# The first four blocks in chunks of 64, with earlier weight loads and a product on two blocks' columns

## The chip, the cores and the metric

The kernel runs on one core of a Trainium2 chip. The metric is the device time of one execution in microseconds (us). The engines of the core work side by side, each from its own queue: PE (TensorE; matmuls, with the weight loads shown as PEld), DVE (VectorE), ACT (ScalarE), POOL (GpSimd), and SP, which issues most of the DMA transfers. They wait for one another by semaphores.

## The reference

```python
# q, k, v: (batch 8, heads 8, seq 576, head_dim 64)
scores = scale * np.matmul(q, k.transpose(0, 1, 3, 2))
gamma = 1.0 - 2.0 ** (-5.0 - np.arange(H, dtype=np.float32))
Dmat = np.where(rel >= 0, gamma[:, None, None] ** rel[None, :, :], 0.0)   # rel = row - column
attn = np.matmul(scores * Dmat[None], v)
x = attn.transpose(0, 2, 1, 3).reshape(B * S, H * D)                       # (4608, 512)
h = np.maximum(np.maximum(x @ w1, x @ w2), x @ w3)                         # d_ff 768
out = h @ w_out                                                            # (4608, 512)
```

The four weight matrices come as 64-bit floats and are turned into 32-bit floats on the chip; q, k and v are 32-bit. No softmax is taken, so attention can be run as a recurrence: a block of tokens needs its own scores and a state, the decayed sum of key times value over all earlier tokens of its sequence.

## The kernel before

**Tiling.** The 4608 tokens are cut into 36 blocks of 128 tokens, four to a tile of 512 (CPT is 4). `ffn(t)` turns the xT of a tile (the attention's result, transposed, 512 columns) into outputs. The hidden size of 768 is six pieces of 128 columns (fb), taken as three pairs (fp). A unit is a pair and one of w1, w2, w3, in the order (fp, i) = (0, 0), (0, 1), (0, 2), (1, 0) and so on. Tile 0 uses plain products: `up_plain(t, h, fb, i)` multiplies one weight piece by the 512 columns of xT in four matmuls, and `maximum` takes the result to h, on ACT for w1 and on DVE, as a maximum, for w2 and w3. Later tiles use formulas with fewer products, which the change does not touch.

**Attention of a block, first four blocks.** `load` fetches k, q and v (256 KB each, SP's queue). `decay` multiplies v by a factor for each row into vd, on POOL for blocks 0 to 2 and on DVE for block 3. `transposes` makes kT and qT on PE, and ACT copies them out of PSUM. `scores` multiplies whole blocks of 128 by 128 for each head (L308); DVE multiplies by the causal mask (st, L311). `state` forms the key-value sums of the block (kv, L421); `keep` adds the old state and multiplies by a factor (L429 to L432). `values` multiplies the masked scores by vd (L462) and adds the old state times q (L477); `output` scales the result into xT on DVE. Helper `soon` runs the DVE steps, so those show line L220.

**Attention of blocks 4 to 7.** `parity_scores` and `parity_values` split a block into two chunks of 64 tokens, and the heads by parity, so that all products are 64 by 64 by 64 (L321, L326, L504, L495). There are two states to a block, the one after its first chunk (mids) and the one after its second (states). The products with the old state are issued in two halves, `old(0)` and `old(1)`. Between them, ACT copies one column of each of the two PSUM tiles into a scrap tile `first` (L508), which holds `old(1)` back until `old(0)` has landed. These four blocks have their place between the products of tile 0.

**Weights.** `load_weights(n)` issues the next n pieces, two DMAs of 256 KB each. `convert_all` is a generator which turns pieces into 32-bit floats in small steps; `convert(n)` runs its next n steps. For a piece they are exponent (one step on DVE, L773, one on ACT, L775), fraction (L781, L782, L784), whole (L787), sign and product (L791, L799; only then may PE use it). The first pair goes piece by piece; the second and the third do exponent and fraction of both pieces first, then whole, sign and product of each; from the fourth on, a pair is one operation.

**Order.** The order on every engine is written out by hand: an engine's queue is the order in which the program issues. The opening (from L1056) loads in the order block 0, block 1, k and q of block 2, piece 0, v of block 2, k and q of block 3, piece 1, v of block 3, then four pieces, and works through blocks 0 to 3. `first_ups`, the first unit of tile 0, contains the rest of block 3: it issues the first piece of w1 on the 384 columns of blocks 0 to 2, then block 3's key-value sums and values, then the second piece on 384 columns, then both on the last 128.

Of the kernel before, what the change touches and what calls it, by code (L numbers as in the profile page):

```python
# [48 lines left out]
C = 128  # L49
# [49 lines left out]
def kernel(  # L99
# [160 lines left out]
    def decay(g):  # L260
        factor = gk[:].unsqueeze(2).to_broadcast([C, H, D])
        t = raws.pop(("v", g))
        if spread or g >= CPT + 2:
            vds[g] = t
            scaling.extend(partial(nc.scalar.mul, t[:, h, :], t[:, h, :], gk[:, h:h + 1]) for h in range(H))
            return
        vds[g] = vpool.tile([C, H, D], FP32, tag="s", name="vd")
        engine = nc.gpsimd if g < CPT - 1 else nc.vector
        engine.tensor_tensor(vds[g][:], t[:], factor, op=ALU.mult)
# [4 lines left out]
    def transposes(g, names="kq"):  # L274
# [14 lines left out]
        for n in names:  # L289
            src = raws["k", g] if n == "k" else raws.pop(("q", g))  # L290
            pool, tag = (ps_r, "r") if g >= CPT else (ps_x, "x")
# [5 lines left out]
    def scores(g):  # L297
        chore(len(urgent))
        scale(len(scaling))
        if g >= CPT:  # L300
            (chunk_scores if g >= BY_CHUNKS else parity_scores)(g)
            return
        qT, kT = qks[g]["q"], qks[g]["k"]
        s = [ps_r.tile([C, NP, C], FP32, tag="r", name=f"s{j}") for j in range(2)]
        for p in range(NP):
            for j in range(2):
                r = slice(D * j, D * (j + 1))
                nc.tensor.matmul(s[j][:, p, :], lhsT=kT[r, p, :], rhs=qT[r, p, :], start=True, stop=True)  # L308
        for j in range(2):
            st = sts[g, j] = att.tile([C, NP, C], FP32, tag=f"m{j}", name="st", bufs=2 + j)  # L310
            soon(partial(nc.vector.tensor_tensor, st[:], s[j][:],  # L311
                         causal[:].unsqueeze(1).to_broadcast([C, NP, C]), op=ALU.mult))

    def parity_scores(g):

        qT, kT, kr, vd = qks[g]["q"], qks[g]["k"], raws.pop(("k", g)), vds[g]
# [7 lines left out]
        def key_value(p, j, c):  # L324
            if c in kept:
                nc.tensor.matmul(rows[c][half(j), 1, p, :], lhsT=kr[half(c), 2 * p + j, :],  # L326
                                 rhs=vd[half(c), 2 * p + j, :], start=True, stop=True)

        for p in range(NP):
            for n in range(2):  # L330
                score(p, 0, n)
                score(p, 1, 1 - n)
                key_value(p, 1 - n, 0)
                key_value(p, n, 1)
# [21 lines left out]
        for c in kept:  # L356
            (states if c else mids)[g + c] = ppool.tile([P, NP, D], FP32, tag="part", name="state")
            soon(partial(keep_parity, c))

    def begins(g):  # L360
        return g + 1 < NG and start_of(g + 1) != 0
# [51 lines left out]
    def state(g):  # L413

        kr = raws["k", g]
        kvs[g] = None
        if begins(g):
            r = start_of(g) or 0
            kvs[g] = ps_r.tile([P, NP, D], FP32, tag="r", name="kv")
            for h in range(H):  # L420
                nc.tensor.matmul(kvs[g][half(h % 2), h // 2, :], lhsT=kr[r:, h, :], rhs=vds[g][r:, h, :],  # L421
                                 start=True, stop=True)

    def keep(g):
        factor = gs[:].unsqueeze(2).to_broadcast([P, NP, D])

        def step(t, kv):
            if start_of(g) is not None:
                nc.vector.tensor_tensor(t[:], kv[:], factor, op=ALU.mult)  # L429
            else:  # L430
                nc.vector.tensor_tensor(t[:], kv[:], states[g][:], op=ALU.add)
                (nc.gpsimd if g < CPT - 2 else nc.vector).tensor_tensor(t[:], t[:], factor, op=ALU.mult)  # L432

        if begins(g):
            t = states[g + 1] = ppool.tile([P, NP, D], FP32, tag="part", name="state")
            soon(partial(step, t, kvs[g]))

# [6 lines left out]
    def values(chunks, new_states=(), later=False, middle=()):  # L444

        def before(g):
            return C if start_of(g) is None else start_of(g)

        chore(len(urgent))
        t, i = divmod(chunks[0], CPT)
        if chunks[0] >= CPT:
            (chunk_values if chunks[0] >= BY_CHUNKS else parity_values)(chunks, t, i)
            return
        pool, tag = (ps_r, "r") if chunks[0] >= CPT - 1 else (ps_y, "y")
        o = [pool.tile([P, len(chunks), NP // 2, C], FP32, tag=tag, name="o") for _ in range(2)]
        for m, g in enumerate(chunks):
            for n in range(NP):
                for c in range(2):  # L460
                    h = head(c, n)
                    nc.tensor.matmul(o[n % 2][half(c), m, n // 2, :], lhsT=vds[g][:, h, :],  # L462
                                     rhs=sts[g, h % 2][:, h // 2, :], start=m == 0 and n < 2,
                                     stop=before(g) == 0, skip_group_check=True)
        for g in new_states:
            if g not in kvs:
                state(g)
        for step in middle:
            step()
        for m, g in enumerate(chunks):  # L470
            old = before(g)
            if old > 0:
                for n in range(NP):
                    for c in range(2):
                        h = head(c, n)
                        r = half(h % 2)
                        nc.tensor.matmul(o[n % 2][half(c), m, n // 2, :old], lhsT=states[g][r, h // 2, :],  # L477
                                         rhs=qks[g]["q"][r, h // 2, :old], start=False, stop=True,
                                         skip_group_check=True)
        finish = partial(output, chunks, o, t, i)  # L480
        if later:
            return finish
        finish()

    def parity_values(chunks, t, i):
        o = [ps_r.tile([P, len(chunks), NP, D], FP32, tag="r", name="o") for _ in range(2)]
# [20 lines left out]
        for m in range(2):  # L507
            nc.scalar.copy(first[:], o[m][:, 0, 0, 0:1])  # L508

        def rest():  # L510
            old(1)
            between.append(partial(chunk_output, o, chunks, t, i))

        between.append(rest)
# [22 lines left out]
    def chunk_output(o, chunks, t, i):  # L537
# [3 lines left out]
        for m in range(2):  # L541
            soon(partial(nc.vector.tensor_tensor, x[:, :, :, m], o[m][:],
                         gq[:, :, half(m)].unsqueeze(1).to_broadcast([P, 2, NP, D]), op=ALU.mult))
        sums_of_x(t, i + len(chunks) - 1)

    def output(chunks, o, t, i):
        if i == 0:
            xT[t] = xpool.tile([P, NDC, NT], FP32, tag="xT", name="xT")
        for b in range(2):
            shape = [P, NP // 2, len(chunks), C]  # L550
            soon(partial(
                nc.vector.tensor_tensor,
                xT[t][:, b::2, i * C:(i + len(chunks)) * C].rearrange("p u (m c) -> p u m c", c=C),
# [651 lines left out]
```

## Time and profile before

| | us |
|---|---|
| median of 3 runs (lowest, highest) | 741.54 (741.34, 741.76) |
| the profiled execution | 741.6 |
| its span in the trace | 739.6 |
| PE busy | 734.1 |
| DVE busy | 576.1 |
| ACT busy | 345.0 |
| PE's first product of the second unit, from the span's start | 30.82 |

The profile comes from one execution. Its own time is 2.0 us longer than the span of the instructions in the trace. Busy times of the engines overlap, so they don't add up to the span. A row of a timeline has the start, the time to the end of the last instruction merged into it, the engine, the line, the operation, what it writes and reads, and how many instructions it stands for. A 32-bit matmul of the program shows as two instructions on PE, called passes here. Times within the text are from the start of the span.

### The profile page before, as it was taken

The page shows a single profiled execution, that of the slowest core. Times are in us where ns is not written, and L with a number is a line of the kernel's source. Part 1 is how long each engine was busy: PE and PEld are TensorE (multiplying, and loading weights), DVE is VectorE, ACT ScalarE, POOL GpSimd, SP SyncE. Part 2 cuts the span into 40 slices and gives each one's busy share as a digit, 9 for nine tenths or more (in the row PEclk, how much of TensorE's full clock was granted, in tenths as well). Part 3 has the DMA queues.
Part 4 walks back from the last instruction along what each step waited for, and adds up shares of the span by engine and source line. Part 5 has one row for each costly group of instructions (what it writes and reads, how often), then busy time and mean ns, then how long its engine had stood idle before and what let it go on. Part 6 is the DMA issues. An engine that isn't in the chain of part 4 may idle for free.

```text
span 739.6 us, 17315 instructions
## 1 busy us (share of the span) xinstructions
PE 734.1 (99%) x6948; PEld 605.8 (82%) x6948; DVE 576.1 (78%) x1066; ACT 345.0 (47%) x731; POOL 33.8 (5%) x42
## 2 busy tenths in 40 slices
PE   8999999999999999999999999999999999999998
PEld 7654556888888888888888888888888888888887
DVE  5998897999886895699668876787768966893676
ACT  4674824454245534544354525543455255424441
POOL 2000000102000100000000000000100010000000
PEclk9999999999999999999999999999999999999999
DMA  9999533415242515141424243332514151000001
GB/s 209 249 245 268 116 59 83 89 21 96 66 85 42 97 36 105 39 83 44 109 51 75 49 107 60 59 58 58 115 22 95 39 106 30 1 31 29 0 1 57
DMA packets 226640, 58.85 MB, mean 80 GB/s; under 512 B 207872, under 2 KB 225280, under 8 KB 226560
## 3 DMA queue, kind: packets, MB, share of 16 engines
q1 hardware_dynamic: 225584, 57.71, 35.8%
q8 instruction: 54, 0.88, 0.5%
q14 instruction: 26, 0.21, 0.1%
q10 hardware_dynamic: 976, 0.04, 0.1%
HBM read 48.27 MB, written 9.44 MB: 78 GB/s over the span
## 4 chain that ended last, share of the span: by engine, by line
PE 97%; SPq 1%; DMA 1%; DVE 0%; issue 0%
PE a L905 20%; PE b L905 17%; PE c L905 9%; PE up L930 8%; PE di L750 7%; PE d L905 6%; PE e L905 6%; PE dhc L750 5%; PE deg L750 3%; PE sk L376 3%; PE down L917 3%; PE o L526 2%; PE dfd L750 2%; PE o L533 2%; PE dx L657 1%; SPq L258 1%
## 5 line engine op out<-in xcount | busy, mean ns | idle before, releaser
L893 DVE TENSOR_TENSOR part<-part 128x512 f32<-128x512 f32 x168 | 117.8, 701 | 86.2 <-ACT part L890 83.6
L890 ACT COPY part<-b 128x512 f32<-128x512 f32 x120 | 70.4, 586 | 163.5 <-PE b L905 163.5
L893 DVE TENSOR_TENSOR h<-h,part 128x512 f32<-128x512 f32 x120 | 83.2, 693 | 24.5 <-ACT h L890 20.5
L890 ACT COPY part<-a 128x512 f32<-128x512 f32 x96 | 56.3, 586 | 51.6 <-PE a L905 51.1
L208 ACT ACTIVATE vraw<-vraw,gk 128x64 f32<-128x64 f32 x240 | 76.8, 347 | 0.1
L905 PE MATMUL b<-s,n 128*128 128x256 f32 x288 | 73.9, 379 | 0.0
L930 PE MATMUL up<-xT,w 128*128 128x512 f32 (+2 forms) x160 | 64.2, 554 | 0.0
L905 PEld LDWEIGHTS b<-s,n 128*128 128x128 f32 x288 | 54.7, 190 | 7.4
L930 PEld LDWEIGHTS up<-xT,w 128*128 128x128 f32 x160 | 28.5, 190 | 29.4 <-issue 26.3
L905 PE MATMUL c<-xT,w 128*128 128x256 f32 x192 | 51.2, 389 | 0.0
L739 ACT COPY k<-di 128x256 f32<-128x256 f32 x49 | 18.2, 372 | 68.4 <-PE di L750 43.4
L905 PE MATMUL d<-s,w 128*128 128x256 f32 x192 | 49.8, 380 | 0.0
L905 PE MATMUL a<-xT,w 128*128 128x256 f32 x192 | 49.3, 379 | 0.0
L905 PE MATMUL b<-xT,n 128*128 128x256 f32 x192 | 49.3, 379 | 0.0
L905 PE MATMUL a<-s,w 128*128 128x256 f32 x192 | 49.3, 379 | 0.0
L393 POOL TENSOR_TENSOR s<-s,gs_of 64x512 f32<-64x512 f32 x21 | 22.5, 1072 | 558.1 <-DVE s L391 441.7
L905 PE MATMUL e<-xT,w 128*128 128x256 f32 x192 | 45.4, 379 | 0.0
L905 PE MATMUL a<-xT,n 128*128 128x256 f32 x192 | 45.4, 379 | 0.0
L905 PEld LDWEIGHTS e<-xT,w 128*128 128x128 f32 x192 | 36.5, 190 | 5.4 <-issue 0.5
L905 PEld LDWEIGHTS a<-xT,w 128*128 128x128 f32 x192 | 36.5, 190 | 5.0
L905 PEld LDWEIGHTS a<-s,w 128*128 128x128 f32 x192 | 36.5, 190 | 5.0
L905 PEld LDWEIGHTS b<-xT,n 128*128 128x128 f32 x192 | 36.5, 190 | 5.0
(200 smaller groups left out, 1378.2 us busy)
## 6 DMA issues: line engine op xcount, KB each, us to landing
bits<-in_moe_w_dram SPq DMA_DIRECT2D x36, 256.0 KB, 5.7
kraw<-in_k_dram SPq DMA_DIRECT2D x32, 256.0 KB, 3.1
vraw<-in_v_dram SPq DMA_DIRECT2D x32, 256.0 KB, 3.5
qraw<-in_q_dram SPq DMA_DIRECT2D x224, 32.0 KB, 2.1
kxraw<-in_k_dram SPq DMA_DIRECT2D x224, 32.0 KB, 2.1
out_dram<-osb SPq DMA_DIRECT2D x56, 128.0 KB, 1.7
bits<-in_moe_w_out_dram SPq DMA_DIRECT2D x6, 512.0 KB, 4.9
qraw<-in_q_dram SPq DMA_DIRECT2D x7, 256.0 KB, 5.6
```

The lines of the kernel that those rows point to most:

```text
L208: scaling.popleft()()
L376: nc.tensor.matmul(s[half(c), h, :], lhsT=kT[half(c), h, :], rhs=qT[half(c), h, :], start=True, stop=True)
L393: nc.gpsimd.tensor_tensor(new, new, factor, op=ALU.mult)
L526: nc.tensor.matmul(o[m][half(c), n, u, :], lhsT=vds[g][half(m), h, :], rhs=sts[g][half(m), h, :], start=n == 0 and u == 0, stop=place(g, m ...
L533: nc.tensor.matmul(o[m][half(c), n, u, :], lhsT=stacks[g][half(m), h, :], rhs=qks[g]["q"][half(m), h, :], start=False, stop=True, skip_gro ...
L739: nc.scalar.copy(place, a)
L750: nc.tensor.matmul(banks[chain], lhsT=hidden(h, order, b, late_ones)[:, e], rhs=late["V"][v][:, e], start=begins and e == 0, stop=chain no ...
L890: nc.scalar.copy(of[step], ps[step[0]][:])
L893: nc.vector.tensor_tensor(of[dst], a, b, op=op)
L905: nc.tensor.matmul(ps[chain][:, e, :], lhsT=factor(w, 2 * fp + e), rhs=xS[t][x], start=n == 1 and e == 0, stop=ends, skip_group_check=True)
L917: nc.tensor.matmul(b[:], lhsT=h[:, fb, m * P:(m + 1) * P], rhs=w_sb["out", fb], start=fb == blocks[0], stop=fb == blocks[-1])
L930: nc.tensor.matmul(ps[:, a:b], lhsT=w_sb[i, fb][:, dc * P:(dc + 1) * P], rhs=xT[t][:, dc, a:b], start=dc == 0 and a == 0, stop=dc == NDC - ...
```

## The change

It makes four alterations, all ahead of the second unit of tile 0.

1. Blocks 0 to 3 use `parity_scores` and `parity_values`, as blocks 4 to 7 do; the old `scores`, `state`, `keep`, `output` and their helpers are gone. For these blocks, scores and key-value products are issued apart: `parity_scores` issues all scores and their masks and returns `state`, which issues the key-value products and the updates of the state when it is called. `parity_values` returns its second half (`old(1)` and the writes of xT) in the same way, and its copies into `first` are made by DVE instead of ACT.
2. vd of block 0 is made by DVE instead of POOL. Transposes of block 3 use the other PSUM pool.
3. The first weight piece is loaded ahead of block 2, the second ahead of block 2's v, the third ahead of block 3's v. The second pair of pieces is converted piece by piece, like the first.
4. The first product of the first piece is made on 256 columns (blocks 0 and 1), in the middle of block 2's work; 128 columns follow after block 2, and the second piece's 384 columns come ahead of block 3's key-value sums.

```diff
-        engine = nc.gpsimd if g < CPT - 1 else nc.vector
+        engine = nc.gpsimd if 0 < g < CPT - 1 else nc.vector
 ...
-            pool, tag = (ps_r, "r") if g >= CPT else (ps_x, "x")
+            pool, tag = (ps_r, "r") if g >= CPT - 1 else (ps_x, "x")
 ...
+        order = [(p, n) for p in range(NP) for n in range(2)]
+        for p, n in order:
+            scored(p, n)
+            if g >= CPT:
+                summed(p, n)
 ...
+        def state():
+            for p, n in order:
+                summed(p, n)
+            keep()
+        return state
 ...
         old(0)
         for m in range(2):
-            nc.scalar.copy(first[:], o[m][:, 0, 0, 0:1])
+            (nc.vector.tensor_copy if t == 0 else nc.scalar.copy)(first[:], o[m][:, 0, 0, 0:1])
         def rest():
             old(1)
-            between.append(partial(chunk_output, o, chunks, t, i))
+            if t == 0:
+                chunk_output(o, chunks, t, i)
+            else:
+                between.append(partial(chunk_output, o, chunks, t, i))
+        if t == 0:
+            return rest
         between.append(rest)
 ...
-        two = Two(0)
-        for e in TWO:
+        for n in range(2):
+            two = Two(n)
+            for e in TWO:
 ...
-        for n in (1, 2):
+        for n in (2,):
 ...
     def first_ups(h):
         g = CPT - 1
-        rest0, copy0 = up_plain(0, h, 0, 0, g * C)
-        convert(2)
-        state(g)
-        convert(2)
-        values([g])
-        keep(g)
-        convert(2)
-        rest1, copy1 = up_plain(0, h, 1, 0, g * C)
-        convert(2)
-        for step in (rest0, copy0, rest1, copy1):
-            step()
-        convert(4)
+        rest0, last0, copy0 = up_plain(0, h, 0, 0, 2 * C, g * C)
+        transposes(g, "k")
+        state()
+        output = values([2])
+        transposes(g, "q")
+        convert(1)
+        output()
+        convert(1)
+        following = scores(g)
+        rest0()
+        last1, copy1 = up_plain(0, h, 1, 0, g * C)
+        convert(2)
+        decay(g)
+        following()
+        output = values([g])
+        convert(1)
+        output()
+        convert(1)
+        for step in (last0, copy0, last1, copy1):
+            step()
+        convert(6)
 ...
     load(1)
+    load_weights(1)
     load(2, "kq")
     load_weights(1)
     load(2, "v")
     load(CPT - 1, "kq")
     load_weights(1)
     load(CPT - 1, "v")
+    load_weights(1)
     load_weights(2)
-    load_weights(2)
-    decay(0)
 ...
+    decay(0)
     transposes(0)
     warm(2)
 ...
-    scores(0)
-    state(0)
-    transposes(1)
     decay(1)
-    first_output = values([0], [0], later=True)
-    keep(0)
-    scores(1)
-    first_output()
-    state(1)
-    transposes(2)
+    state = scores(0)
+    transposes(1, "k")
+    state()
+    transposes(1, "q")
+    output = values([0])
+    state = scores(1)
+    output()
+    state()
+    convert(2)
+    output = values([1])
+    transposes(2, "k")
+    output()
+    convert(1)
+    transposes(2, "q")
+    convert(1)
     decay(2)
-    keep(1)
+    state = scores(2)
     convert(2)
-    values([1], [1])
-    scores(2)
-    convert(2)
-    transposes(CPT - 1, "k")
-    state(2)
-    values([2], [2], middle=[partial(transposes, CPT - 1, "q")])
-    keep(2)
-    convert(2)
-    scores(CPT - 1)
-    decay(CPT - 1)
```

## The prediction

> **What bounds the kernel now.** I read the page first, then the waits of PE (TensorE's matmuls), then the timeline of the opening, since the diff touches only what is issued before the second unit of up products.
>
> ```profile
> PE 734.1 (99%) x6948; PEld 605.8 (82%) x6948; DVE 576.1 (78%) x1066; ACT 345.0 (47%) x731; POOL 33.8 (5%) x42
> PE   8999999999999999999999999999999999999998
> DVE  5998897999886895699668876787768966893676
> ```
> ```profile
> PE kt L294 <- DMA kraw<-in_k_dram: 0.7, 1, 0.7
> PE s L308 <- ACT qT L295: 0.2, 1, 0.2
> PE o L462 <- DVE xT L220: 0.2, 1, 0.2
> ```
>
> PE is busy for 99% of the span, and once the opening is over it waits for nothing that counts. So whatever moment PE reaches the steady row of `up` products is carried to the end: a microsecond lost or won in the opening is one in the total. The windows view gives PE 23.79 us busy in the first 26.20, and full windows up to 300 us. PE's timeline of the end of the opening:
>
> ```profile
> 21.19 2.85 PE L930 MATMUL up<-xT,w 128*128 128x384 f32 x8
> 24.12 0.69 PE L421 MATMUL kv<-vd,kraw 128*64 128x64 f32 x16
> 24.64 1.05 PE L462 MATMUL o<-st,vd 128*64 128x128 f32 x16
> 25.61 0.67 PE L477 MATMUL o<-qT,state 64*64 64x128 f32 x16
> 26.21 15.17 PE L930 MATMUL up<-xT,w 128*128 128x384 f32 x48
> ```
>
> After block 3 there are still 2.7 us of products of the second piece of w1 (384 columns) behind which DVE writes block 3's xT: that handoff is hidden. The next unit starts when its weight is converted, just in time:
>
> ```profile
> 30.07 0.69 DVE L799 TENSOR_TENSOR w<-mant,expo 128x512 f32<-128x512 f32 x1
> 30.82 0.30 PEld L930 LDWEIGHTS up<-xT,w 128*128 128x128 f32 x2 [0.17 <-DVE w L799]
> ```
>
> I measure the change by this start, 30.82 us. ("w2, first piece" below is the first 128 hidden columns of the second matrix, of which this is the start.)
>
> **What the Trainium skill says.** "TensorE: Matmul & The Clock Gate", Part 3, The mechanism: products in different tiles of the array overlap. The trace agrees: 64x64 products cost 0.034 us each (two passes), the 128-column scores of L308 0.14 each. "PSUM — Partial Sum Buffer", PSUM bank collisions: two engines must be kept apart by bank and quadrant, not by address. New here: scores and key-value sums share a bank, so the key-value products wait for both masks. Same page, Engine vs sequencer instructions: VectorE and ScalarE queues are strict FIFO. DVE's rows stand in issue order in this trace. "TensorE: Matmul & The Clock Gate", Why this matters for your kernels: idle gaps above some 3 us slow PE's clock; my longest new gap is 1.0 us, so I charge nothing (the trace shows a granted clock of 1.00 throughout).
>
> **PE, cheaper.** From the second four blocks, which already work by parity:
>
> ```profile
> 76.54 1.16 PE L504 MATMUL o<-m,vd 64*64 64x64 f32 x64
> ```
> ```profile
> 66.47 0.75 DVE L337 TENSOR_TENSOR m<-s,low 128x256 f32<-128x256 f32 x2
> 67.14 0.87 DVE L345 TENSOR_TENSOR state<-s,state 128x256 f32<-128x256 f32 x2
> 68.04 0.42 DVE L347 TENSOR_TENSOR state<-state,gs 128x256 f32<-128x256 f32 x1
> ```
>
> A block costs PE 16 scores, 16 key-value products, 16 values: 0.55 each stretch, and old state 0.31 twice: 2.3 us. Before: 1.09 (L308), 0.61 (L421), 1.02 (L462), 0.60 (L477): 3.3. PE saves 1.0 a block, some 4 in all. Scores alone, or key-value products alone, stand in no row: at the low end they pack as the mixed ones do (0.55, which I take: four neighbours in issue order lie in four tiles), at the high end a stretch takes the 1.08 that 24 mixed ones took from 49.06 on; on the path that is 0.5 more in blocks 2 and 3.
>
> **DVE, dearer and on the path.** A block: masks 0.75 (before 1.29), state 1.33 (before 0.41 to 0.83, one multiplication of 0.61 on POOL), xT 0.75 (same), and two one-column copies `first`, which ACT makes later in the kernel in 0.16 each; on DVE no row shows them. "VectorE: DVE Perf Modes", The TRN2 errata, gives 120 cycles and the columns at 0.96 GHz out of PSUM: an estimate of 0.13. I take 0.36 for the pair; the ends are 0.25 and 0.5. vd of block 0 moves from POOL to DVE: 0.68, in DVE's idle stretch 6.26 to 7.63: nothing. POOL keeps vd of blocks 1 and 2 (1.04 to 1.19 each), done by 10.2 and 18.6, wanted at 11.3 and 20.4: nothing. The second half of the old state (`rest`) waits for these copies, which stand in DVE's queue behind the state updates. So a block is now a relay: key-value products, state, copies, old state, xT, next product.
>
> **The relay, with times.** Up to PE's first scores (6.4) nothing changes. Each landing is 0.27 us of product tail and 0.06 of semaphore.
> - Block 0: scores to 7.25, masks to 8.05, key-value to 8.85, state to 9.75; its last multiplication waits for gs (lands 9.93, as before), to 10.4; copies to 10.7. Block 1: scores end 10.8 (behind a qT copy), masks to 11.6, key-value to 12.4, state to 13.75.
> - DVE then has exponent and fraction of w1's first piece, 0.67, and the copies, to 14.7. PE old state to 15.35, xT to 16.1, whole, sign and product of that piece 2.0: 18.05. Before, it was ready at 19.83.
> - `up` on 256 columns: 8 passes of 0.215 (between 0.112 for 128 and 0.322 for 384), to 19.85. k transposes to 20.35, key-value of block 2 to 21.2, state to 22.55, copies to 22.85, old state to 23.5, xT to 24.3.
> - 128 columns more: 8 x 0.112, to 25.25. w1's second piece is only ready at 25.6 (sign and product behind xT); its 384 columns, 8 x 0.322, to 28.25.
> - Key-value of block 3 to 29.1, state to 30.4, copies to 30.7, old state to 31.3, xT to 32.1. Nothing is left for PE meanwhile: 0.9 us of it idle before `rest`, 0.8 before xT. Then 128 columns of both pieces, 2 x 0.9: 34.0. w2's first piece is ready at 33.4.
>
> So 34.0 for 30.82. The same additions over the kernel before give 31.0, so I take 0.2 off: **+3.0**.
>
> **Two weights come late behind it.** Before, ACT's three conversions for w2's second piece start at 27.79, ahead of its two copies to h; now they are issued behind the copies, which wait for the last `up`: copies to 34.8, then 0.78 + 0.72 + 0.72, to 36.9; sign and product on DVE 1.4: 38.4. PE has done the first piece (3.43) at 37.4: **+1.0** (before: ready 32.69, wanted 34.24). From there DVE's list to the first piece of w1's second pair is the old one, 11.96 us (32.69 to 44.65, almost without idle): 50.35. PE wants it after 3 x 3.43 and 0.9 of transposes, 49.65: **+0.7** (before: 44.65 against 45.53). Afterwards DVE has idle stretches again (57.30 to 58.19), and the delay grows no more.
>
> **Loads.** SP's queue of 256 KB transfers: w1's first piece moves from places 9, 10 to 7, 8, its second from 14, 15 to 11, 12, w2's first from 17, 18 to 16, 17. k, q of block 2 go to 9, 10, v to 13, k, q of block 3 to 14, 15, v to 18. By place, landings before were 10.7, 11.8, 12.8, 15.2, 15.7, 16.5, 17.4, 19.2, 20.1, 21.7, 23.5, 24.6 (7th to 18th). By these k of block 3 lands 19.2, wanted 19.85; q 20.1, wanted 22.0; v 24.6, wanted 26.9; w1's first 11.8, wanted 13.7. Each is covered by the relay, so earlier weights win nothing; if the relay is 1 us quicker than I say, k and v of block 3 bind instead.
>
> **Sum.** 3.0 + 1.0 + 0.7 = 4.7; I take 4.6. The profiled execution took 741.6 (span 739.6 and 2.0 around it), the median is 741.54, no difference to speak of: **746.1**.
>
> **Rivals.**
> - Weights catch up (0.20): the relay costs 3.0, but the two stalls close. For: they rest on margins of 1.0 and 0.7. Against: ACT's order is fixed. 741.5 + 3.0 = 744.5.
> - PE's saving counts (0.05, the other side): DVE's updates and copies fall behind products, not in front of them. Place: DVE's queue from block 2's state to w2's product. PE 4 us lighter would meet w2's first piece, which lands at 23.5 at best and needs v of block 3 (24.6), xT at about 27.6 and 1.4 for sign and product: 29.0, 1.8 earlier, 739.7. It decides if xT of block 3 is written before 28.9, that is 3.2 us before my 32.1. For: before, PE was idle for only 2.4 us of the opening. Against: each step above waits by a semaphore.
> - No difference (0.05): half of that gain, 740.6.
> - The loads come later too (0.10): a transfer on a slow queue, as w1's 15.2 before, puts k or v of block 3 behind my times by 1.5 us; or the small products cost their high end: 747.8.
>
> **Numbers.** My forecast has 0.60. It is 744.9 to 747.2 alone (0.25 us per block for the copies and handoffs); with the catch-up and late loads 743.3 to 748.2. A difference below 0.2% (1.5 us) can't be told from none.
>
> **What would show it.** Right: PE waits on DVE of 0.5 to 1 us before the second half of the old state (`first`), one before the last 128 columns (xT), and two on w near 37 and 50 us; the steady `up` row about 3 us later; DVE's gaps in the opening end on PE. Wrong: w2's first product before 31 us; or waits on DMA there, in which case the loads bind and my relay is too slow.

## The result and the profile after

The changed kernel took 751.46 us (median of four runs: 749.32, 751.45, 751.46, 751.48), beside 741.60 for the kernel before on the same chip. The ratio is 1.0126, with a 95% interval of 1.0108 to 1.0144. The prediction was 746.1, with a range of 743.3 to 748.2: slower, as it said, but by 9.9 us instead of 4.6, and outside its range.

First the page of the kernel after, PE's row and the row of the granted clock:

```profile
PE 737.5 (98%) x7212; PEld 608.4 (81%) x7212; DVE 578.9 (77%) x1081; ACT 344.9 (46%) x731; POOL 31.6 (4%) x40
PEclk9899999999999999999999999999999999999999
```

PE has 264 instructions more than before (7212 for 6948: 64 by 64 products are more and smaller), and one slice of the clock row shows 8 where the kernel before had only nines. The profiled execution took 751.45 us, so it stands for the median; its span is 749.7 us, for 739.6 before.

PE's waits in the kernel after (engine, line and what it waited for: us in total, times, longest):

```profile
PE o L441 <- DVE first L454: 4.2, 4, 2.7
PE up L871 <- DVE w L739: 1.5, 3, 0.7
PE up L871 <- DVE xT L220: 1.1, 2, 0.9
```

These are the waits that the prediction named (copies, xT, weights), but one wait for the copies is 2.7 us long, where 1.0 was the longest forecast. PE's timeline of the opening of the kernel after shows where (start, time, line, how many; idle time before it):

```profile
10.04 0.69 PE L309 MATMUL s<-qT,kT 64*64 64x64 f32 x32
13.48 0.45 PE L441 MATMUL o<-qT,state 64*64 64x64 f32 x8 [2.75 <-DVE first L454]
...
20.95 3.75 PE L871 MATMUL up<-xT,w 128*128 128x256 f32 x8
...
36.15 0.46 PE L441 MATMUL o<-qT,state 64*64 64x64 f32 x16 [0.87 <-DVE first L454]
37.49 5.49 PE L871 MATMUL up<-xT,w 128*128 128x128 f32 x24 [0.88 <-DVE xT L220]
43.70 7.13 PE L871 MATMUL up<-xT,w 128*128 128x512 f32 x16 [0.72 <-DVE w L739]
```

Two things stand out. The gap of 2.75 us is in block 0, ahead of its second old state. And the product on 256 columns takes 3.75 us for its eight passes, where I had reckoned 1.72, or some 2.0 with the tail of the last pass. The row at 37.49 holds the last 128 columns of both pieces and then w2's first piece: the measure of the prediction, PE's first product of the second unit, is 16 passes of 0.112 behind it, at 39.3, for 30.82 before.

What block 0 waits for is seen in the answer for the tile gs, the decay factors of the state (1 KB each in two DMAs on ACT's queue), in the kernel after:

```profile
  DMA gs<-in_state_decay_dram: 2.9, 1
DMA to landing us min/median/max: 3.7/4.9/6.1
```

DVE's last multiplication of block 0's state waits 2.9 us for it, and the copies stand behind it. The second gs transfer took 6.1 us. The same answer of the kernel before:

```profile
DMA to landing us min/median/max: 3.5/3.5/3.5
```

Last, the windows view of the kernel after, in stretches of 3.41 us counted from the places where the record of the granted clock changes (us; busy time and instruction count of PE, PEld, DVE, ACT, POOL; granted clock; DMA share; GB/s):

```profile
8.58:11.99 3.41, 2.16 (x90) 1.78 (x80) 0.85 (x2) 0.59 (x2) 1.04 (x1) 1.00 1.08 255
11.99:15.41 3.42, 1.93 (x78) 1.76 (x79) 2.41 (x9) 0.77 (x1) 0.00 (x0) 1.00 0.78 208
15.41:18.82 3.41, 3.16 (x46) 2.39 (x38) 2.44 (x9) 1.92 (x3) 1.28 (x2) 0.50 1.19 258
18.82:22.23 3.41, 2.69 (x37) 2.08 (x36) 3.22 (x8) 1.40 (x3) 0.00 (x0) 0.50 1.04 230
```

By the record of the clock PE had half of it from 15.41 to 25.65, which is three stretches of 3.41 us, right after one in which it was busy for 1.93 of 3.42.

Behind this the relay went as forecast: from block 2's last 128 columns (29.43) on, every step lies 5.1 to 5.4 us behind its forecast time. So the theory with which I went into the first experiments, called A there, was: the forecast's own steps hold, and the missing 5.3 us are the late gs and the half clock that its gap brings.

### The profile page after: what moved, and what is told of

Same layout as the page of the kernel before. It is cut to its first block, busy times and chain, and to the rows that moved or that the text cites. A ratio compares the mean times of both kernels' runs of the same rounds, so it can differ in the third digit from the quotient of the medians.

```text
span 749.7 us, 17859 instructions
## 1 busy us (share of the span) xinstructions
PE 737.5 (98%) x7212; PEld 608.4 (81%) x7212; DVE 578.9 (77%) x1081; ACT 344.9 (46%) x731; POOL 31.6 (4%) x40
## 4 chain that ended last, share of the span: by engine, by line
PE 94%; DMA 2%; DVE 1%; SPq 1%; ACT 1%; issue 0%; DVEq 0%; ACTq 0%
PE a L846 19%; PE b L846 17%; PE c L846 9%; PE di L690 6%; PE up L871 6%; PE d L846 6%; PE e L846 6%; PE dhc L690 5%; PE deg L690 3%; PE sk L382 3%; PE down L858 3%; PE o L477 2%; PE dfd L690 2%; PE o L484 2%; PE dx L597 1%; DMA bits<-in_moe_w_dram 1%
## 5 line engine op out<-in xcount | busy, mean ns | idle before, releaser
L871 PE MATMUL up<-xT,w 128*128 128x512 f32 (+3 forms) x168 | 66.8, 550 | 2.7 <-DVE w L739 1.5
L871 PEld LDWEIGHTS up<-xT,w 128*128 128x128 f32 x168 | 30.2, 197 | 32.4 <-issue 25.5
```

The source lines that it names most:

```text
L871: nc.tensor.matmul(ps[:, a:b], lhsT=w_sb[i, fb][:, dc * P:(dc + 1) * P], rhs=xT[t][:, dc, a:b], start=dc == 0 and a == 0, stop=dc == NDC - ...
```

## The experiments

Each kernel is the kernel after with the edit shown, or the one that it names. The kernel before had medians of 741.2 to 741.6 beside them.

**gs earlier.** Only the issue of gs is moved, on ACT's queue, up behind that of gk.

```diff
     nc.scalar.dma_start(gk[:], key_decay)
+    for j in range(2):
+        nc.scalar.dma_start(gs[half(j)].unsqueeze(2), state_decay[half(j), :, D * j:D * j + 1])
...
     warm(2)
-    for j in range(2):
-        nc.scalar.dma_start(gs[half(j)].unsqueeze(2), state_decay[half(j), :, D * j:D * j + 1])
```

> The kernel after, with the two transfers of gs issued on ACT's queue right behind that of gk instead of behind block 0's transposes. After: 751.46 us, gs lands at 12.55, PE then waits 2.75 us for the first copies of block 0, and the clock record shows half clock from 15.41 to 25.65. Theory A (the 5.4 us that the forecast missed are the late gs, some 2.7, and the half clock that its gap brings, some 2.5): gs lands before 9, the wait before the second old state of block 0 falls under 0.9, the clock stays at 1.00, and the time is 746.1 (745 to 747). Theory B (the half clock comes from PE being sparse in the whole opening, not from that gap): 2.7 less only, 748.8, and half clock still there. Theory C (the loads set the opening, weights ahead of k and q of block 2): the gap moves behind a transfer, 750.5 to 751.5.

Measured: 749.83 us (748.39 to 750.38; ratio to before 1.011, 1.0095 to 1.0125). The gap in block 0 is gone, but only 1.6 us came back. The time lies above theory B's 748.8 and below C's 750.5; the half clock is still there, as B had it. PE's waits of this kernel, and two of its windows with the clock:

```profile
PE up L873 <- DVE w L741: 2.4, 3, 1.7
...
PE o L452 <- issue: 1.0, 1, 1.0
```
```profile
16.29:19.70 3.41, 1.07 (x35) 0.76 (x34) 3.38 (x7) 1.47 (x3) 2.05 (x2) 1.00 0.84 196
19.70:23.12 3.42, 3.42 (x10) 2.60 (x10) 1.02 (x4) 1.44 (x2) 0.00 (x0) 0.50 1.14 278
```

The half clock is still there, later: it follows a stretch in which PE was busy for 1.07 of 3.41, and falls on the 256-column product once more (3.58 us). A second one came at 36.77, after 1.67 of 3.41. And a wait of 1.0 us appears that has no releaser ("issue"), in block 1. So A was incomplete: half clock comes without the wait for gs too, with no gap above 1.7 us, and another wait had stood behind gs.

**The gap filled.** gs stays late; products on a constant tile fill PE's wait.

```diff
     state = scores(1)
+    fill(22)
     output()
```

> The kernel after, with 22 products of 128 columns on a constant tile (results not used) issued on PE between block 1's scores and the second old state of block 0, where PE waits 2.75 us for gs; nothing else is moved, so gs stays late. Theory A: the clock stays at 1.00, the state of block 0 is as late as before, so only the half clock's share comes back: 749.0 (748.4 to 749.5). Theory B (sparse PE in the whole opening): the half clock comes later or stays, 750.5 to 751.5. If the half clock costs nothing, because the relay's waits hide it: 751.5.

Measured: 753.62 us (752.73 to 754.57), outside everything that was expected. I had sized the filling wrongly: a product of the program is two passes, so 22 of them took 5.18 us and themselves made the relay 2.6 us later. The run is still of use for the clock. From the timeline of its PE:

```profile
22.95 1.96 PE L877 MATMUL up<-xT,w 128*128 128x256 f32 x8 [0.86 <-DVE w L745]
...
37.21 7.12 PE L877 MATMUL up<-xT,w 128*128 128x128 f32 x24 [0.88 <-DVE xT L226]
```

At full clock the 256 columns take 1.96 us. The half clock came in 37.45 to 40.86, after the waits for block 3, and made 24 passes take 7.12 us where the kernel after took 5.49.

**The old order of loads.**

```diff
-    load_weights(1)
     load(2, "kq")
...
-    load_weights(1)
+    load_weights(2)
     load_weights(2)
```

> The kernel after, with the order of the loads of the kernel before (first piece of w1 behind k and q of block 2, the second piece's place as before). Theory A: gs lands at 9.9 as in the kernel before, no gap above 1 us in block 0, clock at 1.00; the first piece of w1 lands at 12.8 and 15.2 and is ready at about 18 to 18.5, where the relay wants it at 18.0: 746.3 (745.5 to 747.5). Theory C' (the earlier weights are needed by the new order of work): PE waits for w1 by 1 to 2 us more, 748 to 749. If gs is late for another reason than the weights ahead of it: 751 to 752.

Measured: 750.92 us (750.25 to 751.31; 1.0112 to 1.0142). gs took 3.1 and 3.4 us, and DVE waited 0.3 for it: so it is the weights ahead of it that delay gs in the kernel after. The time can't be told from that of the kernel after, and the same two things are there as with the early gs: "issue" of 1.56 us in block 1, and half clock from 17.12 to 23.95.

**The loads alone, in the kernel before.** The same lines changed the other way.

> The kernel before, with the load order of the kernel after and nothing else. Theory A: gs lands at about 12.5 instead of 9.93, the state of block 0 is written at 13.0 instead of 10.5, DVE's masks of block 1 behind it are 1.8 late, and PE's values of block 1 (13.08 before) start at about 14.5; w1 lands earlier, and part of this is taken back: 742.5 (741.5 to 743.5), with a PE gap under 2.5 us and the clock at 1.00. If the gap is as long as that in the kernel after and brings half clock: 744 to 745. If the load order is free: 741.5.

Measured: 742.99 us (742.67 to 743.89; ratio 1.0024, 1.0014 to 1.0034), as theory A had it in time. But PE's waits show another cause than late masks:

```profile
PE kt L294 <- DMA kraw<-in_k_dram: 2.0, 2, 1.2
PE qt L294 <- DMA qraw<-in_q_dram: 0.5, 2, 0.3
```

Weights that land earlier put k and q of blocks 2 and 3 later, and PE waits for these. DVE also waited 2.3 us for gs here, but what showed on PE was the loads. So the change's order of loads costs 1.5 us in the kernel before. In the new opening no cost of it can be told (751.46 and 750.92, with runs that overlap).

**PE kept busy in the relay.** From here on with the early gs. Products on the constant tile go into four of PE's waits.

```diff
+    fill(2)
     state = scores(2)
...
+        fill(6)
         rest0, last0, copy0 = up_plain(0, h, 0, 0, 2 * C, g * C)
...
+        fill(3)
         output()
+        fill(3)
```

> The kernel of the early gs (749.83), with products of 128 columns on a constant tile (0.235 us each, results not used) in PE's waits: two ahead of block 2's scores, six ahead of the 256-column product, three ahead of the second old state of block 3 and three behind it. Each lies in a wait that the trace of the early gs shows (0.68, 1.66, 0.86, 0.88), so they take no time themselves. Theory A (PE's clock is halved for the 3.41 us that follow a window of 3.41 us in which PE was busy for half or less, and that costs what the products of that window take longer): the clock stays at 1.00 to the end, the 256-column product takes 1.9 instead of 3.58, and of the second half-clock window (36.8 to 40.2) 0.9 is won, since the wait for w2's second piece that it hid comes back: 747.2 (746.6 to 748). If the half clock only fills time in which PE would wait for DVE: 749.5 to 750.

Measured: 747.57 us (747.45 to 747.76; ratio 1.0086, 1.0069 to 1.0103), so 2.3 less by work that computes nothing. The clock is 1.00 up to the end. That half clock costs time is borne out: PE does more, and the kernel is faster. From PE's timeline:

```profile
19.57 1.97 PE L879 MATMUL up<-xT,w 128*128 128x256 f32 x8 [0.23 <-DVE w L747]
...
33.83 5.49 PE L879 MATMUL up<-xT,w 128*128 128x128 f32 x24
40.03 7.13 PE L879 MATMUL up<-xT,w 128*128 128x512 f32 x16 [0.72 <-DVE w L747]
```

The last 128 columns start at 33.83, for 35.61 with the early gs alone, 37.49 in the kernel after, and 32.15 in the forecast.

**The copies ahead of the second update of the state** (with PE kept busy).

```diff
-                soon(partial(keep_parity, c))
+                if c and g < CPT:
+                    after_first[g] = partial(keep_parity, c)
+                else:
+                    soon(partial(keep_parity, c))
...
             (nc.vector.tensor_copy if t == 0 else nc.scalar.copy)(first[:], o[m][:, 0, 0, 0:1])
+        if t == 0 and chunks[0] in after_first:
+            after_first.pop(chunks[0])()
```

> The one with the filled waits, and in blocks 0 to 3 the update of the second half's state (addition 0.45, multiplication 0.42) issued on DVE behind the two first copies instead of ahead of them. Theory A (the relay runs through DVE's queue, and the copies' place in it sets when PE goes on): the wait for the copies in block 3 goes from 0.86 to some 0.4, but xT still stands behind all of it: 0.3 to 0.8 less than the one with the filled waits. If DVE's updates weigh fully (0.87 in each of blocks 2 and 3): 1.7 less. If they lie beside other work: no change.

Measured: 749.27 us (747.77 to 749.69), 1.7 more. In the profiled run the half clock was back for 3.41 us, and the waits for the copies turned into waits for xT (0.62 and 0.45 us). The half clock isn't all of it: of the three other runs, whose mean clock was 0.999 or 1.000, two took 749.0 and 749.5, and the best, 747.77, lies beside the 747.45 to 747.76 of the kernel that it is to be compared with. DVE's row of block 3 shows a cost of the order itself:

```profile
33.28 0.42 DVE L466 COPY first<-o 128x1 f32<-128x1 f32 x2 [0.55 <-PE o L453]
```

DVE now stands idle for 0.55 us ahead of the copies, where it had updated the second half's state before, and in blocks 2 and 3 each it is 4.25 us from the key-value products to the next `up` (31.56 to 35.81 in block 3), for 3.88 to 3.89 with PE kept busy. So the order of the kernel after is the better one.

**Conversion steps ahead of the copies to h** (with PE kept busy).

```diff
-        convert(1)
+        convert(3)
         for step in (last0, copy0, last1, copy1):
             step()
-        convert(6)
+        convert(4)
```

> The one with the filled waits, and the first two conversion steps of w2's second piece issued ahead of the last 128-column products and the two copies to h instead of behind them. My step of the two late weights (waits on w of 0.72 and 0.52 in the kernel after; forecast 1.0 and 0.7): both waits go, 1.2 less than the one with the filled waits (0.9 to 1.6). If DVE, not ACT's order, holds these weights: no change, or 0.3 less.

Measured: 745.74 us (745.68 to 746.47; ratio 1.0064, 1.0049 to 1.0079), 1.8 less. Both waits for weights are gone from PE's timeline, which now runs through:

```profile
33.23 12.35 PE L879 MATMUL up<-xT,w 128*128 128x128 f32 x40
```

The two waits had been 0.72 and 0.51. The 1.8 us are above the range given, and the other 0.6 isn't the edit's as far as the profile shows: in the profiled run the opening was that much earlier, ahead of anything that was moved (33.23 for 33.83). The record of the clock has it at full from 4.91 us on here, and from 6.08 with PE kept busy; block 0's scores start at 6.41 and 6.77. My step of the two late weights is confirmed in its cause, and within 0.5 us in its size.

**No product on two blocks' columns** (with PE kept busy): 384 columns at once behind block 3's scores.

```diff
-        fill(6)
-        rest0, last0, copy0 = up_plain(0, h, 0, 0, 2 * C, g * C)
...
-        rest0()
+        last0, copy0 = up_plain(0, h, 0, 0, g * C)
```

> The one with the filled waits, and the first product not begun on 256 columns ahead of block 2's key-value products: 384 columns at once behind block 3's scores (the six products that filled the wait ahead of it left out as well). PE's work is the same. Theory A: the relay of block 2 starts about 2 us earlier, since PE no longer stands in the 1.7 us wait for w1 and in 1.9 us of products ahead of it, and the product of 128 columns becomes one of 384 behind it: within 0.7 us of the one with the filled waits. If the product on two blocks' columns hides the relay as it is placed to: 1.5 to 2 us more. If it only stands in the relay's way: 1.5 to 2 us less.

Measured: 747.71 us (747.15 to 748.28), the same as 747.57, as theory A had it in time. Without the split PE comes to block 3's k transposes earlier, and waits for the load:

```profile
PE kt L302 <- DMA kraw<-in_k_dram: 1.8, 1, 1.8
```

The split product costs nothing and wins nothing that shows; it stands where PE would otherwise wait for k of block 3. Two of the four runs, the profiled one among them, had a stretch of half clock (mean clock 0.998) and took 748.2 and 748.3; the two at 1.000 took 747.2. So one such stretch went with 1.0 us here.

**The copies on ACT** (with the conversions first).

```diff
-            (nc.vector.tensor_copy if t == 0 else nc.scalar.copy)(first[:], o[m][:, 0, 0, 0:1])
+            nc.scalar.copy(first[:], o[m][:, 0, 0, 0:1])
```

> The one with the conversions first (745.74), and the first copies of blocks 0 to 3 on ACT, as in the later blocks (0.16 each), instead of on DVE (0.41 a pair). If DVE's queue is what the relay runs through, each of blocks 2 and 3 is 0.4 quicker to its xT, and block 1 by the same before w1's first piece is ready: 744.8 (744.4 to 745.3). If PE's products, or the conversions' own chain, bind there: 745.7.

Measured: 746.60 us (746.18 to 747.54), 0.9 more. Block 2 became quicker: from its key-value products to its 128 columns it is 3.60 us (23.02 to 26.62), and 3.89 with the copies on DVE (21.30 to 25.19). Block 3 did not: from block 2's 128 columns to the last ones it is 8.05 us (26.62 to 34.67), and 8.04 with the copies on DVE (25.19 to 33.23). But there PE goes straight from the products that fill its wait, which were sized for copies on DVE, to the second old state:

```profile
32.40 0.94 PE L183 MATMUL warm<-spreader 128*128 128x128 f32 x6
33.26 0.46 PE L449 MATMUL o<-qT,state 64*64 64x64 f32 x16
```

The copies had ended at 32.86, so what they won is hidden by the filling. In block 1 the copies now stood in ACT's queue behind conversion steps:

```profile
PE o L449 <- ACT first L462: 1.3, 1, 1.3
```

and the half clock followed, from 15.63 to 19.05. A miss in time: what block 2 won was less than what block 1 lost. Of block 3 this kernel says nothing.

**Without two warming products** (with the conversions first). In the kernels where gs comes in time, PE stopped in block 1 with no releaser. The hardware_dynamic queues of the page carry data; its "instruction" queue q8 moved 0.92 MB in 56 packets, 16 KB each. In each of these kernels the trace has PE going on 1.3 to 1.6 us after such a packet had come in (at 12.60 with the early gs, where PE goes on at 14.13). The kernel before has 54 such packets. That goes with PE's own program: 7212 matmuls and as many weight loads in the kernel after, 6948 of each before, both some 257 instructions to a packet. Two products fewer ahead of it move any place of PE's program by eight instructions.

```diff
     transposes(0)
-    warm(2)
```

> The one with the conversions first, without the two warming products ahead of block 0's scores: 4 matmul records and 4 weight loads fewer in PE's program. In every kernel with an early gs PE stops after the 13th record of block 1's values, for 0.85 to 1.6 us, with no releaser, and goes on 1.4 to 1.6 us after a 16 KB packet of the instruction queue has come in. If PE waits for that block of its instructions, the stop lies at a fixed place of the program and comes 8 instructions later in the work: after the 17th record of these values. If it waits for data (masks, vd, a PSUM buffer), it stays after the 13th. Time: within 0.5 us of the one with the conversions first.

Measured: 746.07 us (745.65 to 747.17), no difference. Block 1's values in the kernel with the conversions first, and then in this one:

```profile
12.06 0.58 PE L458 MATMUL o<-m,vd 64*64 64x64 f32 x13
13.50 0.50 PE L458 MATMUL o<-m,vd 64*64 64x64 f32 x18 [0.85 <-issue]
```
```profile
12.53 0.59 PE L458 MATMUL o<-m,vd 64*64 64x64 f32 x17
14.36 0.40 PE L458 MATMUL o<-m,vd 64*64 64x64 f32 x12 [1.23 <-issue]
```

The stop moved from behind the 13th record to behind the 17th, as expected if it lies at a fixed place of the program; for a wait for data no move was expected. So PE waits for its instructions there; why it goes on only 1.3 to 1.6 us after the packet, no run shows.

**The product behind block 3's relay.** With the copies on ACT, the second piece's 384 columns come behind block 3's second old state; block 3's masks are issued ahead of the piece's sign and product, and its vd is made on POOL.

```diff
-        engine = nc.gpsimd if 0 < g < CPT - 1 else nc.vector
+        engine = nc.gpsimd if 0 < g < CPT else nc.vector
...
         output()
-        convert(1)
         following = scores(g)
+        convert(1)
         rest0()
-        last1, copy1 = up_plain(0, h, 1, 0, g * C)
-        convert(2)
         decay(g)
         following()
         output = values([g])
-        convert(1)
-        fill(3)
+        convert(2)
         output()
-        fill(3)
-        convert(3)
+        last1, copy1 = up_plain(0, h, 1, 0, g * C)
+        convert(4)
```

> The one with the copies on ACT, and in block 3 the 384 columns of w1's second piece placed behind the second old state instead of ahead of the key-value products, with what these need brought forward: block 3's masks ahead of the second piece's sign and product on DVE, vd of block 3 on POOL; the last six filling products left out. Theory A (PE's saving is lost in the relay, and comes back as far as other products stand behind it): the last 128-column products start 1.4 earlier, since the waits for the copies and xT lie beside 2.75 us of products: 743.5 (742.8 to 744.5). If v and k of block 3 (last landing 24.3) or POOL bind: no change, 744.8. If it had to be under the kernel before to count as a gain, both would have to be 2 us better than that: not expected.

Measured: 745.92 us (744.58 to 746.13), 0.7 less than with the copies on ACT, and above the range given: in the profiled run block 1 lost 1.5 us behind ACT's queue, and the half clock came in 17.94 to 21.35.

**The same with the copies on DVE.**

> As the one with the product behind, but with the first copies back on DVE: on ACT they stood behind conversions in block 1 (PE waited 1.5 us for them there, and the half clock followed). In the conversions-first kernel the 256-column product starts at 18.97, and in the product-behind one 12.5 us lie between that start and the last 128-column products, against 14.3 in the former. Theory A (both hold when put together): the last 128-column products start at 31.5, and the time is 744.1 (743.5 to 745.0), so 1.6 less than the conversions-first kernel; still 2.5 to 3 above the kernel before, since blocks 1 and 2 keep their relay and PE its wait for instructions. If the gain of the product behind came from the copies on ACT in block 3: 745.5.

Measured: 744.62 us (744.00 to 744.97; ratio 1.0043, 1.0026 to 1.0060), 1.1 less than with the conversions first, within the range given for theory A. PE's timeline from block 3's second old state:

```profile
28.75 0.46 PE L449 MATMUL o<-qT,state 64*64 64x64 f32 x16 [0.87 <-DVE first L462]
29.15 14.93 PE L879 MATMUL up<-xT,w 128*128 128x384 f32 x48
```

The wait for xT lies beside the 384 columns now, and with their 2.75 us the last 128 columns start at 31.9, for 31.5 expected. In this profiled run block 1 had no stop for instructions, but a wait of 0.9 us for the copies came in its place: the 256-column product starts at 18.97, as in the profile with the conversions first, and the gain of 1.3 (31.9 for 33.23) is made behind that. It is the best version of the changed opening, 6.8 us better than the kernel after, and still 3.2 slower than the kernel before. None beat the kernel before.

## Why the prediction was wrong, step by step

The measure is the start of the last 128-column products, which the forecast put at 32.15 (xT at 32.1 and a semaphore) and the kernel after has at 37.49.

| kernel | gs wait in block 0 | half clock ahead of it | stop for instructions | start |
|---|---|---|---|---|
| forecast | none | none | none | 32.15 |
| after | 2.75 | 10.24 | none | 37.49 |
| gs early | none | 3.41 | 1.0 | 35.61 |
| gs early, PE kept busy | none | none | 1.0 | 33.83 |

- **Block 0, "its last multiplication waits for gs (lands 9.93, as before)": failed.** This is the first step that broke. gs landed at 12.55, so the copies came at 13.0 to 13.4 instead of 10.7, and PE's next step 2.7 us late. The "Loads" part reckoned the landings of SP's queue by place, and took gs, on ACT's queue, as untouched. It isn't: the profile counts the packets of both queues on the same 16 DMA engines, and the change puts 256 KB weight transfers ahead of block 2. With the old order of loads gs took 3.1 and 3.4 us again.
- **Clock, "my longest new gap is 1.0 us, so I charge nothing": failed.** The premise fell with gs. But the reading was wrong too, as the kernel with gs early shows: with no gap above 1.7 us it had half clock twice. Not one gap counts, but a stretch of 3.41 us in which PE has little to do. The forecast itself had waits of 0.9 and 0.8 us in block 3 and should have asked. Half clock costs what the products of that stretch take longer: 1.8 us for the 256 columns (3.75 or 3.58 for 1.97), less where PE would wait anyway.
- **The relay, "+3.0": right in kind, short by 1.7 us.** With gs early and PE kept busy, the last 128 columns start at 33.83 for the forecast's 32.15. 1.5 of it is there when the 256-column product starts (19.57 for 18.05). Some 0.5 stands when block 1's xT is written (16.64 for 16.1), behind the stop for instructions of 1.0, which no row of the kernel before shows and part of which fell into other waits; 0.85 is DVE's sign step of w1's first piece, 1.54 us for 0.69, while POOL made vd of block 2. In the kernel after these two don't show: with gs late, PE began block 1's values only at 14.67, when the stop of the other kernels was over (14.13 with gs early), and DVE to the sign step at 19.39, when POOL had ended at 18.32. That is why taking gs away moved the 256-column product by only 1.4 (20.95 to 19.53). No kernel was built to take away the meeting with POOL alone.
- **PE, "0.55 each stretch": right.** Block 3's key-value products take 0.52 us to the next row and its values 0.48 (33.60, 34.12 and 34.60 in the kernel after): alone they pack as closely as mixed. What PE saved stood in waits.
- **The waits in block 3, "0.9 before `rest`, 0.8 before xT": right**, 0.87 and 0.88. Also the copies: DVE's row has 0.41 us for the pair, for the 0.36 taken.
- **Cause of the waits, "copies, which stand in DVE's queue behind the state updates": half right.** They do stand there. Moving them ahead of an update won nothing, since DVE then waits for the first old state. On ACT they made block 2 quicker by 0.3, and with the product behind, the wait ahead of block 3's second old state was 0.50 us with the copies on ACT and 0.87 on DVE; but the time was worse for it both times, as block 1 lost more.
- **Two weights late, +1.0 and +0.7: right**, 0.72 and 0.52 in the kernel after, and both gone with the conversions issued ahead of the copies to h. ACT's timeline of the kernel after has them one behind the other:

```profile
39.58 0.59 ACT L878 COPY h<-up 128x512 f32<-128x512 f32 x1 [0.31 <-PE up L871]
40.06 0.77 ACT L715 ACTIVATE mant<-bits,one 128x512 f32<-128x512 uint32 x1
```

- **Loads, "each is covered by the relay, so earlier weights win nothing": right for k and v of blocks 2 and 3** in the kernel after, where PE waits for none of them in the opening. The margin was small, as the kernel without the split shows (1.8 us of waiting for k).
- **The sum.** 8.5 at w2's first piece (39.3 for 30.82) and 1.2 for the two weights make 9.7 of the 9.9 measured. The forecast had 3.0 and 1.7 there. The term that was mis-sized is the first, by 5.4. Of these, 2.7 are the wait for gs as it stands in the kernel after. From the start of the 256-column product to the last 128 columns the kernel after takes 16.54 us (20.95 to 37.49), and the two kernels with full clock there, gap filled and PE kept busy, take 14.26 each (22.95 to 37.21, 19.57 to 33.83), for 14.1 in the forecast. So the half clock costs 2.3 there, 1.8 of it in the 256 columns. Some 0.4 isn't placed.
- **The rivals.** "PE's saving counts" was refuted on its own term: xT of block 3 was not written before 28.9. "The loads come later too" (747.8, with 0.10; 746.1 and its 1.5 us make 747.6) had the right direction for a wrong transfer: not k or v of block 3, but one of 1 KB.

With gs early, the clock kept up and the stop for instructions as it is, the kernel takes 747.6; that is the prediction's model with its missing 1.5. What remains open: what the half clock of the kernel after cost ahead of its 256-column product, since the filling that was to keep the clock with gs late was itself too long there.

## What to carry to other kernels

- When work is made smaller on the engine that bounds, ask what it then waits for: here PE saved work in four blocks and lost more in a relay with DVE, of which each handoff is 0.3 us and DVE's list some 3 us in each of blocks 2 and 3.
- A load order is a schedule for everything on the DMA engines, also for transfers on other queues (gs took 3.5 us before and up to 6.1 after). Look for the smallest transfer that someone waits for, and issue it first.
- Where PE gets sparse, look at the granted clock by stretches, not at the longest gap. Products that compute nothing, in waits that are there anyway, won 2.3 us here; where they are longer than the wait, they cost time instead (22 of them made the relay 2.6 us later), and hide what another edit wins in it.

## What the runs showed of the hardware

- **Half clock without an idle stretch.** "TensorE: Matmul & The Clock Gate" (Part 1, What's actually happening) has the clock halved after an idle window of some 3.4 us, in windows that run freely. The length agrees: every half-clock stretch in these openings is 3.41 us or a multiple. So do the windows: the record's first full clock lies anywhere from 4.1 to 6.9 us of the span, depending on the profile. But PE was never idle for a whole window. Half clock followed stretches with PE busy for 1.07, 1.67, 1.68, 1.69 (twice), 1.74, 1.77, 1.89 and 1.93 of 3.41 us, in the profiles of eight kernels; after 1.76 and 1.80 it stayed at full, so busy time alone is not the measure. After a full-clock stretch with 2.16 or more in the openings it stayed at full. In the kernel after it stayed at half behind stretches with 3.16 and 2.69 busy, and with the copies on ACT it came back behind one with 3.15.
- **A stop for instructions.** "Runtime: NRT & Kernel Launch" (Instruction fetch mechanics) says that engines fetch their instructions in blocks of 16 KiB, mostly hidden. The blocks agree. It was not hidden here: PE stopped for 0.3 to 1.6 us in the opening of nine of the ten kernels with 64 by 64 products where gs came in time, at a fixed place of the program, and went on 1.3 to 1.6 us after the packet's end. In the tenth profile (the product behind, copies on DVE) it did not.
- **A transfer of 1 KB** in 4-byte packets took 3.5 us beside the loads of the kernel before, and up to 6.1 beside the weights.
- **DVE beside POOL.** An operation of DVE with two inputs in SBUF (128 by 512) took 1.41 to 1.54 us instead of 0.69 where POOL's multiplication of vd ran at the same time: in the kernel with PE kept busy, 1.54 at 17.15 with POOL's 1.04 at 17.11. In the same profile, beside POOL's row from 9.59 to 10.64, an update of the state with an input in PSUM kept its 0.42 us (at 9.65), and one with both in SBUF took 0.80 for 0.42 (at 10.11).
